# Pooled attention with a top-1 mixture of experts: the zero rows of dropped tokens move to the front of the expert loop, and two steps of the hand-over change places

## Chip, cores and metric

The kernel runs on one core of one Trainium2 chip. The metric is device time in microseconds of one execution. The time given for a kernel is the median of its runs. Times inside an execution are counted from the start of the profiled span.

## What is computed

Attention over pooled keys and values (pool of 8) gives 4608 rows of 512 numbers. A gate of 8 columns picks one expert for each row. Each expert takes at most `capacity` = 1152 rows, in the order of the rows; a row that comes later is dropped, and its output is zero. Kept rows go through two products with a ReLU between and are scaled by their gate weight.

```python
def _moe_ref(x, w_gate, w1, w2, capacity):
    logits = x @ w_gate
    expert_idx = np.argmax(logits, axis=1)
    ...
    for i in range(N):
        e = expert_idx[i]
        if counts[e] < capacity:
            disp[e, counts[e]] = x[i]
            pos[i] = counts[e]
            counts[e] += 1
            keep[i] = True
    h = np.maximum(np.einsum('ecd,edf->ecf', disp, w1), 0.0)
    y = np.einsum('ecf,efd->ecd', h, w2)
    out = np.zeros((N, D), dtype=np.float32)
    for i in range(N):
        if keep[i]:
            out[i] = gate_w[i] * y[expert_idx[i], pos[i]]
```

## The kernel before, in words

The program has three parts.

**Attention.** It works through units of rows, writes the attention rows to `xs` in device memory, routes them as it goes and scatters pairs (row number, gate weight) into `slots`, which is sorted by expert. It ends at about 209 us of the span.

**The prologue (`prologue`, the hand-over).** The expert that has most rows after half of the batch is known early. Its first 256 rows are computed while the last routing steps and the tables of the loop (`tables`) are still being made. The order of its instructions is written out by hand (a block with a manual schedule: each engine takes its instructions in the order of the source). `product(yp[1], ...)` is split in two halves of 12 matmuls, with the transposes of the next rows (`transposed`) between them on TensorE. `load_w2(e1, nc.scalar)` issues the next expert's w2 on ScalarE's queue. Then VectorE makes two versions of the row list: `idd` (the dropped rows alone; all other entries get the number NT = 4608) and `ids` (the kept rows alone). A scatter with bounds check leaves out an entry of NT. `columns(ix1, ...)` copies the two columns of the first pass, `gather(xg, ix1, ...)` on GpSimd fetches their rows, and `finish(i)` (L986 to L988) multiplies `yp[i]` with the gate weight on VectorE and scatters it from GpSimd. In the loop's own pools, `zi` (zeros) and the PSUM tile `y[1]` are then cleared on VectorE (L1111, L1115). PSUM tile `y[1]` lies on the bank of the prologue's `pa`, whose second half is `yp[1]`.

**The loop (L1158).** 20 passes in this execution, counted from 0 here; the number is read from a register. A pass takes up to 256 rows of one expert, in two tiles of 128. With `two` set both tiles are worked on (15 passes, the long ones: `hidden_all` in four groups of 24 matmuls that take turns over three PSUM buffers `ph`, then `product(y[1], ...)`); otherwise only one (5 passes, the short ones: `hidden_one`). Where the expert changes (`sw`), ScalarE and VectorE split the next expert's w1 and w2 into two parts each (`split_w1`, `split_w2`; `split` puts the high part on ScalarE, the low part on VectorE), and where there is one more expert to come (`nw`), SP loads its weights behind that. The order in a pass, for each engine:

- TensorE: hidden layer, `product(y[1])`, transposes of the rows for the next pass, `product(y[0])`.
- VectorE: `hl` of each group (L1133), the w1 split, `ix` (the two columns of the pass after the next), the two `xl`, `io` (this pass's columns), `gate(1)`, `iz` (this pass's columns of dropped rows, L1183), `gate(0)`, the w2 split, and then `hl` of the next pass.
- GpSimd: it clears `io` (L1167) and `iz` (L1168), gathers `xg` (L89, L91), then reads `iz` once into `guard` (L1184) and scatters `zrow` (a tile of zeros) to the rows in `iz` (two scatters, L96), then scatters `ys[1]` and `ys[0]` to the rows in `io` (L1193, L96).

Clearing an index tile on GpSimd, and reading a tile into `guard` or `guardf`, serve the ordering: an instruction that clears `io` waits until the scatters that read `io` have landed, and VectorE's write of `io` then waits for the clearing alone. The same holds for `iz`. SP stores one row of `zrow` into `xs` ahead of the loop (L1155).

All engines make semaphore events at the loop's entry (L1158); a first-pass instruction that depends on what another engine did before the loop waits for that engine's entry event.

```python
            with tc.manual_schedule():
                ...
                nc.gpsimd.tensor_sub(io, zi, zi)
                nc.gpsimd.tensor_sub(iz, zi[:, 0], zi[:, 0])
                ...
                nc.vector.tensor_scalar(out=iz, in0=idd[:, ds(cd, 2)], ...)
                nc.gpsimd.tensor_sub(guard[:, 0], iz, iz)
                for i in range(2):
                    scatter(iz[:, i : i + 1], zrow[:, :], across_iterations=True)
                product(y[0], hh, hl, 0)
                gate(0)
```

Of the kernel before, what the change touches and what calls it, by code (L numbers as in the profile page):

```python
# [12 lines left out]
I32 = mybir.dt.int32  # L13
# [6 lines left out]
DVE = mybir.EngineType.DVE  # L20

P = 128
# [9 lines left out]
def pooled_attn_top1_moe(ctx: ExitStack, tc: tile.TileContext, q, k, v, wg, w1, w2, cap, out):  # L32
# [7 lines left out]
    nc = tc.nc  # L40
# [40 lines left out]
    idd = const.tile([P, NCOL + 2], I32, name="idd")  # L81
    guard = const.tile([P, 2, 2], I32, name="guard")
    guardf = const.tile([P, 2], F32, name="guardf")

    def columns(dst, src):
        nc.vector.tensor_scalar(out=dst, in0=src, scalar1=0, scalar2=None, op0=ALU.bitwise_or)  # L86
# [29 lines left out]
    def load_w2(e, eng=nc.sync, **kw):  # L116
        for c in range(0, KF, 4):
            eng.dma_start(wr[2][:, c : c + 4], rows(w2f, e * DF + c * P, 4 * P).rearrange("(c p) f -> p c f", p=P), **kw)
# [30 lines left out]
    def product(y, hh, hl, i, first=0, last=3 * KF):  # L149

        terms = [(hh, wr["h"]), (hh, wr["l"]), (hl, wr["h"])]
        for n in range(first, last):
            a, b = terms[n // KF]
            c = n % KF
            nc.tensor.matmul(y, a[:, c, i * P : (i + 1) * P], b[:, c], start=(n == 0), stop=(n == 3 * KF - 1))  # L155


    with ExitStack() as actx:
# [558 lines left out]
        with tc.manual_schedule():  # L717
# [102 lines left out]
            def transposed(i, x):  # L820

                p_ = bank([P, KD, P], "pxe", F32R)
                for c in range(KD):
                    nc.tensor.transpose(p_[:, c], x[:, i, c * P : (c + 1) * P], identr)
                s = (slice(None), slice(None), slice(i * P, (i + 1) * P))
                split(xh[s], xl[s], p_.bitcast(F32))
# [105 lines left out]
            def prologue():  # L932

                hh = ld.tile([P, KF, 2 * P], F32R, name="hh", tag="qblk")
                hl = ld.tile([P, KF, 2 * P], F32R, name="hl", tag="qblk")
                pa = pav.tile([P, 2, 512], F32, name="pa", tag="pa")
                pc = [psc.tile([P, 4, 2 * P], F32, name="ps", tag="ps") for _ in range(2)]
                two = [pc[0][:, 0:2], pc[1][:, 0:2], pa[:, 0].rearrange("p (a n) -> p a n", a=2), pc[0][:, 0:2]]
                ya = wk.tile([P, 2, H, D], F32, name="xo", tag="xo").rearrange("p a h d -> p a (h d)")
                yp = [pc[1].rearrange("p a n -> p (a n)")[:, 0:DM], pa[:, 1]]  # L940

                def hidden(g):
                    hidden_two(g, two[g], xh, xl)

                def relu(g):
                    s = (slice(None), slice(2 * g, 2 * g + 2))
                    nc.scalar.activation(hh[s], two[g], AF.Relu)
                    nc.vector.scalar_tensor_tensor(out=hl[s], in0=two[g], scalar=0.0, in1=hh[s].bitcast(F32), op0=ALU.max, op1=ALU.subtract)

                def w2_piece(c, eng):  # L950
                    s = (slice(None), c)
                    split(wr["h"][s], wr["l"][s], wr[2][s], eng)

                drain(dq)
                e1 = nc.values_load(esi[0:1, 1:2], engines=(SP, mybir.EngineType.Activation), min_val=0, max_val=E - 1)
                load_w1(e1)
                hidden(0)
                for c in range(5):
                    w2_piece(c, nc.gpsimd)
                drain(rq)  # L960
                drain(sq)
                ix = sm.tile([P, 2, 2], I32, name="idp", tag="idp", bufs=2)
                nc.sync.dma_start(ix, slotv[:, ds(early["e0"] * MT + 2, 2), :])
                nc.sync.dma_start(ids[:, 0:NCOL, :], slotv)
                rq.append(tables())
                relu(0)
                hidden(1)
                for c in (5, 6, 7):
                    w2_piece(c, nc.vector)
                    step(rq, 4)  # L970
                relu(1)
                hidden(2)
                step(rq, 10)
                relu(2)
                hidden(3)
                nc.vector.tensor_tensor(out=ix[:, :, 0], in0=ix[:, :, 0], in1=mkeep[:, 2:4], op=ALU.max)
                gather(xg, ix, xs[:, :])
                step(rq, 4)
                relu(3)
                product(yp[0], hh, hl, 0)  # L980
                drain(rq)
                ido = sm.tile([P, 2], I32, name="ido", tag="ido", bufs=1)
                idp = early["id"]
                nc.vector.tensor_tensor(out=ido, in0=idp[:, :, 0], in1=mkeep[:, 0:2], op=ALU.max)

                def finish(i):  # L986
                    nc.vector.tensor_scalar_mul(ya[:, i], yp[i], idp[:, i, 1:2].bitcast(F32))
                    scatter(ido[:, i : i + 1], ya[:, i])  # L988

                product(yp[1], hh, hl, 1, 0, 12)  # L990
                for i in range(2):
                    transposed(i, xg)
                load_w2(e1, nc.scalar)
                product(yp[1], hh, hl, 1, 12, 24)
                nc.vector.tensor_tensor(out=idd, in0=ids[:, :, 0], in1=mdrop, op=ALU.max)
                nc.vector.tensor_tensor(out=ids[:, :, 0], in0=ids[:, :, 0], in1=mkeep, op=ALU.max)
                c1 = nc.values_load(cf[0:1, 3, 1:2], engines=(DVE,), min_val=0, max_val=NCOL)
                ix1 = sm.tile([P, 2, 2], I32, name="ix1", tag="ix1", bufs=1)
                columns(ix1, ids[:, ds(c1, 2), :])
                gather(xg, ix1, xs[:, :])  # L1000
                finish(0)
                finish(1)

            NPU = 2 * NB + 1
# [94 lines left out]
    with ExitStack() as bctx:  # L1099
# [6 lines left out]
        ys = [tb.tile([P, DM], F32, name=f"ys{i}") for i in range(2)]  # L1106
        ix = tb.tile([P, 2, 2], I32, name="ix")
        io = tb.tile([P, 2, 2], I32, name="io")
        iz = tb.tile([P, 2], I32, name="iz")
        zi = tb.tile([P, 2, 2], I32, name="zi")  # L1110
        nc.vector.memset(zi, 0)  # L1111
        px = [pp.tile([P, KD, P], F32R, name=f"px{i}") for i in range(2)]
        ph = [pp.tile([P, 512], F32, name=f"ph{i}") for i in range(3)]
        y = [pp.tile([P, DM], F32, name=f"y{i}") for i in range(2)]
        nc.vector.memset(y[1], 0.0)  # L1115

        def transpose_x():
            for i in range(2):
# [39 lines left out]
        with tc.For_i(0, nt, 1, iteration_sync="reg_based") as t:  # L1158
            with tc.manual_schedule():
# [3 lines left out]
                we = nc.values_load(cf[0:1, 2, ds(t, 1)], engines=(SP,), min_val=0, max_val=E - 1)  # L1163
                ct = nc.values_load(cf[0:1, 3, ds(t, 1)], engines=(DVE,), min_val=0, max_val=NCOL)
                c2 = nc.values_load(cf[0:1, 3, ds(t + 2, 1)], engines=(DVE,), min_val=0, max_val=NCOL)
                cd = nc.values_load(cf[0:1, 4, ds(t, 1)], engines=(DVE,), min_val=0, max_val=NCOL)
                nc.gpsimd.tensor_sub(io, zi, zi)  # L1167
                nc.gpsimd.tensor_sub(iz, zi[:, 0], zi[:, 0])  # L1168
                with tc.If(two > 0) as both:
                    hidden_all()  # L1170
# [10 lines left out]
                columns(io, ids[:, ds(ct, 2), :])  # L1181
                gate(1)
                nc.vector.tensor_scalar(out=iz, in0=idd[:, ds(cd, 2)], scalar1=0, scalar2=None, op0=ALU.bitwise_or)  # L1183
                nc.gpsimd.tensor_sub(guard[:, 0], iz, iz)  # L1184
                for i in range(2):
                    scatter(iz[:, i : i + 1], zrow[:, :], across_iterations=True)
                product(y[0], hh, hl, 0)
                gate(0)
                with tc.If(sw > 0):  # L1189
# [31 lines left out]
```

## Time and profile before

| | us |
|---|---|
| Median of 3 runs | 672.89 (671.79 to 673.55) |
| The profiled execution's own time | 671.99 |
| Its span in the trace | 669.8 |
| TensorE busy (matmuls) | 625.5, 93% of the span |
| VectorE busy | 343.9, 51% |
| GpSimd busy | 310.6, 46% |
| ScalarE busy | 236.8, 35% |
| Mean granted TensorE clock | 0.981 |

The own time is 2.2 us longer than the span: work around the first and the last instruction that the trace does not show. Busy time is the union of an engine's instructions. In the rows, PE is TensorE, DVE VectorE, ACT ScalarE, POOL GpSimd, and a q behind a name is the engine's sequencer; L146 is line 146 of the kernel; `out<-in` are the tiles; what stands in square brackets is the idle time of the engine before the instruction, and what ended it.

### The profile page before, as it was taken

How to read it: one execution, taken by the hardware profiler on the slowest of the kernel's cores; microseconds unless marked ns; L12 is line 12 of the kernel's file. 1: busy time of each engine (PE TensorE's matmuls, PEld its weight loads, DVE VectorE, ACT ScalarE, POOL GpSimd, SP SyncE). 2: the span in 40 equal slices, each digit the busy share in tenths (PEclk: the TensorE clock that was granted, in tenths of full speed). 3: DMA queues.
4: the chain of work that ended last, by engine and by line, in shares of the span. 5: the costliest groups of instructions: out<-in, count | busy, mean ns of one | idle time of the engine just before them, and what ended most of it. 6: DMA issues, size and time to landing. Idle time of an engine off the chain costs nothing. (4 is left out here: it accounts for less than half of the span.)

```text
span 669.8 us, 14743 instructions
## 1 busy us (share of the span) xinstructions
PE 625.5 (93%) x4218; PEld 560.6 (84%) x4219; DVE 343.9 (51%) x783; ACT 236.8 (35%) x401; POOL 310.6 (46%) x467
## 2 busy tenths in 40 slices
PE   2899989999878989999999999999999999999994
PEld 2899879888777878997888899897998978989983
DVE  4466767778778832227826642224622466221222
ACT  2455545556454111215616431124311463111111
POOL 7699952543386323135543444313543056431444
PEclk9799989999899989999999999999999999999998
DMA  9994844344273151014843761101711181110112
GB/s 326 372 385 138 322 158 127 126 155 145 81 244 120 47 192 31 31 63 171 325 152 142 252 253 63 31 31 63 289 63 31 35 300 38 63 31 31 63 47 64
DMA packets 47086, 93.82 MB, mean 140 GB/s; under 512 B 13392, under 2 KB 23632, under 8 KB 47060
## 3 DMA queue, kind: packets, MB, share of 16 engines
q1 hardware_dynamic: 30836, 60.37, 25.9%
q0 software_dynamic: 11392, 21.57, 9.8%
q10 hardware_dynamic: 4832, 11.56, 4.5%
q8 instruction: 13, 0.21, 0.1%
q14 instruction: 13, 0.11, 0.1%
HBM read 132.97 MB, written 31.27 MB: 245 GB/s over the span
## 5 line engine op out<-in xcount | busy, mean ns | idle before, releaser
L1132 ACT ACTIVATE hh<-ph 128x512 fp32r<-128x512 f32 x60 | 35.9, 599 | 181.3 <-PE ph L146 169.7
L1133 DVE SCALAR_TENSOR_TENSOR hl<-ph,hh 128x512 fp32r<-128x512 f32 x60 | 41.0, 691 | 110.8 <-ACT hh L1132 47.6
L146 PE MATMUL ph<-xl,w1h 128*128 128x256 f32 x480 | 76.8, 282 | 2.6 <-DVE io L86 2.6
L146 PE MATMUL ph<-xh,w1h 128*128 128x256 f32 x480 | 76.9, 282 | 2.1 <-DVEq L1158 2.1
L146 PE MATMUL ph<-xh,w1l 128*128 128x256 f32 x480 | 76.5, 281 | 0.0
L155 PE MATMUL y<-w2h,hh 128*128 128x512 f32 x280 | 72.3, 400 | 0.0
L155 PE MATMUL y<-w2h,hl 128*128 128x512 f32 x280 | 71.0, 396 | 0.0
L155 PE MATMUL y<-w2l,hh 128*128 128x512 f32 x280 | 71.0, 396 | 0.0
L146 PEld LDWEIGHTS ph<-xh,w1h 128*128 128x128 f32 x480 | 66.7, 190 | 3.8 <-issue 2.5
L91 POOL DMA_INDIRECT xg<-xs,ix x42 | 41.1, 978 | 61.8 <-PE y L155 52.3
L146 PEld LDWEIGHTS ph<-xl,w1h 128*128 128x128 f32 x480 | 65.4, 189 | 3.3 <-issue 3.3
L146 PEld LDWEIGHTS ph<-xh,w1l 128*128 128x128 f32 x480 | 65.5, 190 | 0.0
L485 PE MATMUL pa<-vbd,pT 96*128 96x146 f32 (+1 forms) x480 | 63.1, 296 | 1.7 <-DVE lt L511 1.5
L155 PEld LDWEIGHTS y<-w2h,hl 128*128 128x128 f32 x280 | 52.6, 188 | 12.7
L155 PEld LDWEIGHTS y<-w2l,hh 128*128 128x128 f32 x280 | 52.6, 188 | 12.7
L89 POOL TENSOR_TENSOR guard<-ix 128x4 int32<-128x4 int32 x21 | 4.1, 197 | 122.6 <-DVE ix L86 77.5
L485 PEld LDWEIGHTS pa<-vbd,pT 96*128 96x128 f32 (+1 forms) x480 | 58.0, 186 | 3.0 <-ACT pT L472 2.4
L155 PEld LDWEIGHTS y<-w2h,hh 128*128 128x128 f32 x280 | 50.0, 188 | 9.4
L1153 DVE TENSOR_SCALAR ys<-y,io 128x512 f32<-128x512 f32 x40 | 30.0, 751 | 48.9 <-PE y L155 43.7
L122 DVE TENSOR_TENSOR xl<-px,xh 128x512 fp32r<-128x512 f32 x40 | 25.7, 685 | 56.4 <-ACT xh L121 56.4
L96 POOL DMA_INDIRECT out_dram<-zrow,iz x40 | 47.4, 1184 | 14.8 <-issue 13.6
L472 ACT COPY pT<-pp 96x384 f32<-96x384 f32 x72 | 33.9, 475 | 45.3 <-PE pp L471 44.2
(256 smaller groups left out, 1095.0 us busy)
## 6 DMA issues: line engine op xcount, KB each, us to landing
r<-in_moe_w_dram SPq DMA_DIRECT2D x84, 1024.0 KB, 10.9
raw<-in_k_dram SPq DMA_DIRECT2D x12, 768.0 KB, 7.4
raw<-in_v_dram SPq DMA_DIRECT2D x12, 768.0 KB, 9.4
xs<-xo ACTq DMA_DIRECT2D x16, 512.0 KB, 2.8
qblk<-in_q_dram SPq DMA_DIRECT2D x14, 512.0 KB, 6.0
raw<-in_moe_w_dram SPq DMA_DIRECT2D x4, 512.0 KB, 5.2
r<-in_moe_w_dram ACTq DMA_DIRECT2D x2, 1024.0 KB, 8.5
qblk<-in_q_dram SPq DMA_DIRECT2D x4, 256.0 KB, 8.1
```

The source lines that it names most:

```text
L89: nc.gpsimd.tensor_sub(guard, ix, ix)
L91: nc.gpsimd.indirect_dma_start(out=dst[:, i, :].bitcast(F32), out_offset=None, in_=src, in_offset=bass.IndirectOffsetOnAxis(ap=ix[:, i, 0: ...
L96: ins = nc.gpsimd.indirect_dma_start(out=out[:, :], out_offset=bass.IndirectOffsetOnAxis(ap=i_, axis=0), in_=src, in_offset=None, bounds_c ...
L122: eng.tensor_sub(lo, src, hi.bitcast(F32))
L146: nc.tensor.matmul(p[:, f2], a[:, c, f * P : (f + 1) * P], b[:, c], start=(f2 == 0 and j == 0 and c == 0), stop=(f2 == 1 and j == 2 and c ...
L155: nc.tensor.matmul(y, a[:, c, i * P : (i + 1) * P], b[:, c], start=(n == 0), stop=(n == 3 * KF - 1))
L472: nc.scalar.copy(self.pT[:, j], pp[0:KC, 0:HC])
L485: nc.tensor.matmul(self.pa[us, j, h0 * XW : (h0 + 2) * XW], self.pT[:, j, c, us], vbd[b % 2][:, cc].rearrange("r a x -> r (a x)"), start=( ...
L1132: nc.scalar.activation(hh[s], p, AF.Relu)
L1133: nc.vector.scalar_tensor_tensor(out=hl[s], in0=p, scalar=0.0, in1=hh[s].bitcast(F32), op0=ALU.max, op1=ALU.subtract)
L1153: nc.vector.tensor_scalar_mul(ys[i], y[i], io[:, i, 1:2].bitcast(F32))
```

## The change

In the prologue, `finish(0)` and the making of `idd`, `ids` and `ix1` move ahead of the transposes, the load and the second half of the product; the gather follows the load; and a copy of the first pass's columns of dropped rows into `iz` is new. `iz` becomes a tile of the outer pool. In the loop, the two scatters of zero rows move from behind `gate(1)` to the pass's front, ahead of the clearing of `iz`, with a one-column memset of `zrow` and two guards (three instructions; the guard of `iz` moves with them). VectorE's write of `iz` stays where it is and takes the columns of the next pass (`t + 1`). `zi` is cleared on GpSimd, and `y[1]` by a ScalarE copy of `zrow`.

```diff
+    iz = const.tile([P, 2], I32, name="iz")
@@ prologue
                 product(yp[1], hh, hl, 1, 0, 12)
-                for i in range(2):
-                    transposed(i, xg)
-                load_w2(e1, nc.scalar)
-                product(yp[1], hh, hl, 1, 12, 24)
+                finish(0)
                 nc.vector.tensor_tensor(out=idd, in0=ids[:, :, 0], in1=mdrop, op=ALU.max)
                 nc.vector.tensor_tensor(out=ids[:, :, 0], in0=ids[:, :, 0], in1=mkeep, op=ALU.max)
                 c1 = nc.values_load(cf[0:1, 3, 1:2], engines=(DVE,), min_val=0, max_val=NCOL)
                 ix1 = sm.tile([P, 2, 2], I32, name="ix1", tag="ix1", bufs=1)
                 columns(ix1, ids[:, ds(c1, 2), :])
+                for i in range(2):
+                    transposed(i, xg)
+                load_w2(e1, nc.scalar)
                 gather(xg, ix1, xs[:, :])
-                finish(0)
+                c0 = nc.values_load(cf[0:1, 4, 0:1], engines=(DVE,), min_val=0, max_val=NCOL)
+                columns(iz, idd[:, ds(c0, 2)])
+                product(yp[1], hh, hl, 1, 12, 24)
                 finish(1)
@@ ahead of the loop
-        iz = tb.tile([P, 2], I32, name="iz")
         zi = tb.tile([P, 2, 2], I32, name="zi")
-        nc.vector.memset(zi, 0)
+        nc.gpsimd.memset(zi, 0)
...
-        nc.vector.memset(y[1], 0.0)
+        nc.scalar.copy(y[1], zrow)
@@ in the loop
-                cd = nc.values_load(cf[0:1, 4, ds(t, 1)], engines=(DVE,), min_val=0, max_val=NCOL)
+                cd = nc.values_load(cf[0:1, 4, ds(t + 1, 1)], engines=(DVE,), min_val=0, max_val=NCOL)
                 nc.gpsimd.tensor_sub(io, zi, zi)
+
+                nc.gpsimd.memset(zrow[:, 0:1], 0.0)
+                nc.gpsimd.tensor_sub(guardf, zrow[:, 0:2], zrow[:, 0:2])
+                nc.gpsimd.tensor_sub(guard[:, 0], iz, iz)
+                for i in range(2):
+                    scatter(iz[:, i : i + 1], zrow[:, :], across_iterations=True)
                 nc.gpsimd.tensor_sub(iz, zi[:, 0], zi[:, 0])
...
                 nc.vector.tensor_scalar(out=iz, in0=idd[:, ds(cd, 2)], scalar1=0, scalar2=None, op0=ALU.bitwise_or)
-                nc.gpsimd.tensor_sub(guard[:, 0], iz, iz)
-                for i in range(2):
-                    scatter(iz[:, i : i + 1], zrow[:, :], across_iterations=True)
                 product(y[0], hh, hl, 0)
```

## Rows read from the trace of the kernel before

**Rows 1.** Busy time by stage: stretch, length, busy us of each engine (instructions), PEclk, DMA.

```profile
238.70:244.30 5.60, 3.51 (x18) 3.53 (x18) 1.97 (x5) 0.00 (x0) 3.85 (x5) 0.70 0.89 310
...
244.30:661.00 416.70, 412.55 (x2585) 365.67 (x2584) 171.84 (x265) 122.35 (x176) 159.92 (x236) 1.00 0.31 108
```

**Rows 2.** What TensorE waits for in the loop: us in total, times, longest.

```profile
PE ph L146 <- DVE io L86: 2.6, 4, 0.9
PE ph L146 <- DVEq L1158: 2.1, 1, 2.1
```

**Rows 3.** TensorE at the hand-over: start us, us, engine, line, operation [idle before].

```profile
236.67 2.04 PE L155 MATMUL pa<-w2h,hl 128*128 128x512 f32 x8
240.80 1.09 PE L146 MATMUL ph<-xh,w1h 128*128 128x256 f32 x4 [2.09 <-DVEq L1158]
```

**Rows 4.** VectorE at the hand-over, in order of time.

```profile
237.59 0.46 DVE L996 TENSOR_TENSOR ids<-ids,mkeep 128x290 int32<-128x290 int32 x1
...
239.43 0.74 DVE L987 TENSOR_SCALAR xo<-pa,idp 128x512 f32<-128x512 f32 x1
...
240.36 0.48 DVE L1115 MEMSET y<- 128x512 f32 x1 [0.17 <-DVE zi L1111]
```

**Rows 5.** The loop's first line: sequencer events, count, ns, first and last start.

```profile
L1158 ACTq EVENT_SEMAPHORE  x2: 17/17/17, 238.2 to 238.3; - x2
L1158 DVEq EVENT_SEMAPHORE  x2: 21/21/21, 240.6 to 240.7; - x2
```

**Rows 6.** Busy time and granted clock (PEclk) behind two stalls of TensorE.

```profile
240.80:244.30 3.50, 3.50 (x17) 3.50 (x18) 0.04 (x1) 0.00 (x0) 2.69 (x3) 0.52 0.88 297
328.50:332.00 3.50, 3.50 (x32) 3.50 (x31) 3.50 (x5) 0.60 (x1) 3.14 (x3) 1.00 1.00 405
```

**Rows 7.** The tail: GpSimd's last scatters and VectorE's last gate.

```profile
652.02 0.99 POOL L96 DMA_INDIRECT out_dram<-ys,io  x1 [2.15 <-issue]
...
661.08 0.75 DVE L1153 TENSOR_SCALAR ys<-y,io 128x512 f32<-128x512 f32 x1 [2.18 <-PE y L155]
...
664.40 0.99 POOL L96 DMA_INDIRECT out_dram<-ys,io  x1 [0.16 <-issue]
```

**Rows 8.** GpSimd across the seam of two usual passes.

```profile
412.55 0.99 POOL L96 DMA_INDIRECT out_dram<-ys,io  x1 [0.16 <-issue]
415.44 0.19 POOL L1167 TENSOR_TENSOR io<-zi 128x4 int32<-128x4 int32 x1 [1.89 <-DMA out_dram<-ys,io]
...
423.82 0.20 POOL L89 TENSOR_TENSOR guard<-ix 128x4 int32<-128x4 int32 x1 [8.01 <-DVE ix L86]
```

**Rows 9.** The scatters' line: issue to landing.

```profile
DMA to landing us min/median/max: 2.1/2.7/8.0
```

**Rows 10.** GpSimd across the seam of passes 2 and 3.

```profile
314.26 1.79 POOL L96 DMA_INDIRECT out_dram<-ys,io  x1 [0.16 <-issue]
...
316.53 1.79 POOL L96 DMA_INDIRECT out_dram<-ys,io  x1 [0.15 <-issue]
323.49 1.15 POOL L1167 TENSOR_TENSOR io<-zi 128x4 int32<-128x4 int32 x1 [5.17 <-DMA out_dram<-ys,io]
```

**Rows 11.** VectorE in pass 3.

```profile
321.10 4.62 DVE L122 TENSOR_TENSOR w1l<-r,w1h 128x1024 fp32r<-128x1024 f32 x4
...
327.85 0.16 DVE L1183 TENSOR_SCALAR iz<-idd 128x2 int32 x1
...
333.11 1.28 DVE L1133 SCALAR_TENSOR_TENSOR hl<-ph,hh 128x512 fp32r<-128x512 f32 x2
```

**Rows 12.** Busy time and DMA share in pass 3.

```profile
325.70:331.80 6.10, 5.32 (x45) 5.14 (x44) 5.99 (x11) 3.19 (x4) 4.80 (x6) 1.00 0.97 352
```

**Rows 13.** TensorE, start of the fourth group of pass 4.

```profile
334.81 0.64 PE L146 MATMUL ph<-xh,w1h 128*128 128x256 f32 x4
```

**Rows 14.** Pass 14: GpSimd's clearing of io, VectorE's write of iz.

```profile
552.99 1.20 POOL L1167 TENSOR_TENSOR io<-zi 128x4 int32<-128x4 int32 x1 [6.35 <-DMA out_dram<-ys,io]
...
556.27 0.16 DVE L1183 TENSOR_SCALAR iz<-idd 128x2 int32 x1
```

## The prediction

> **What bounds the kernel now.** I read the stages first, then what TensorE waits for, then the two seams that the diff touches, then GpSimd's queue inside the loop. In the loop, TensorE is busy 412.6 of 416.7 us at full granted clock [rows 1]: it is the bound there, and whatever leaves it fed costs nothing. Of its few stalls, 2.6 us in four pieces wait for VectorE, and one of 2.1 us stands at the hand-over [rows 2]. So three places can move the end: the hand-over, the tail behind the last matmul, and any pass in which another engine newly makes TensorE wait.
>
> The change removes no matmul and no transfer. Counting the reference's routing over its inputs, one expert of eight is over capacity, with 236 dropped rows; they lie in the column pairs of passes 4 and 5 (counted from 0). All other zero-row scatters carry row numbers out of bounds and write nothing, but are issued and waited for all the same.
>
> **Hand-over.** The last product of the prologue ends at 236.67+2.04 = 238.71; the loop's first matmul starts at 240.80 [rows 3]. In between VectorE runs finish(0), finish(1) and two memsets, having come from the ids [rows 4]; its loop-entry semaphore event comes at 240.7, and TensorE goes 0.1 us later, while ScalarE's entry event was given at 238.3 [rows 5]. From the start of the last VectorE instruction (240.36) to TensorE's start it is 0.44 us: a register load and the events.
> After the change finish(0) (as long as finish(1), 0.74), the two instructions over all ids (0.46 each) and both column copies with their register loads, some 3 us in all, run while TensorE is still at the product. I cost them at nothing; their cover is the product's end at 238.71, and what of them were still to run then would push finish(1) by as much. finish(1) then runs 238.8 to 239.6. By VectorE alone TensorE could start at 238.8+0.44 = 239.2. But y[1] lies over the PSUM tile that finish(1) reads: in the program of before the memset of y[1] waits for finish(1). Now a ScalarE copy has that wait, and TensorE's first matmul waits for ScalarE's entry event as well. The copy starts at about 239.7, so TensorE at about 239.7+0.44+0.15 (one more wait) = 240.3. **Gain 0.5** (bounds 0.4 and 1.6). The zi memset on GpSimd runs behind its scatter and its landing is not awaited by TensorE. The gather and the first scatter go some 3 us earlier on GpSimd; the gather is read only in mid-pass, 15 us on.
> The granted clock: after the 2.1 us idle, TensorE ran 3.5 us at a mean 0.52, almost all of it at the 1.2 GHz level, and made about half of its work [rows 6], so 0.52 costs 3.5x(1-0.52) = 1.7 us. With 1.6 us idle it may stay at 2.4 GHz. I leave this 1.7 in and keep its loss as a bound.
>
> **Tail.** In the last pass the two zero-row scatters stand on GpSimd ahead of the two result scatters; gate(0) ends at 661.08+0.75 = 661.83, but the last result scatter starts only at 664.40 [rows 7]. With the zero rows gone it could start 0.4 us behind gate(0), at 662.2: gain 2.2. It comes later if the gather ahead of it does, which now stands behind the front's chain: zero scatter, landing, clearing of iz. If GpSimd's own 2 us pause ahead of the scatter in the pass before [rows 7] comes again, the chain ends that much later and the gain falls to 0.3. I take the middle, **1.3**.
>
> **The loop's front.** Every pass now issues on GpSimd ahead of the gather: clearing io, zrow memset, two guards, two zero scatters, clearing iz. Clearing iz has to wait until the zero scatters have landed, since they read iz; VectorE's write of iz waits for that clearing, and behind it in VectorE's queue stand gate(0), the w2 split and the next pass's hl. SP's queue is passed by none of it but the one-row store of zrow, which the memset of the first pass awaits; nothing hurries there.
> In a usual pass there is room: clearing io 2.9 us behind the last result scatter, and 8 us more until the gather's guard gets its ix [rows 8]; the chain needs three reads of 0.2, two scatters 1.3 apart and a landing of 2.7, the median [rows 9], some 5 us. Free, therefore, in 18 passes: the long ones, and the short ones whose front is not under a weight load.
> Pass 3 is short and follows a pass whose w2 load delays the result scatters. Its io clearing waits until 323.49, which is 7.0 us after the second scatter at 316.53; the one that is left at 314.26 lands, by the same 7.0, at 321.3 [rows 10]. From there VectorE splits w1 from 321.10 to 325.7 [rows 11], and GpSimd's clearing took 1.15 there instead of 0.19 [rows 8, 10]. Three reading instructions: 321.3+3.45 = 324.7; two scatters of about 1.4 with 0.3 between: the second starts at 326.6.
> Its landing is not in the trace of before. The bounds are the median of 2.7 and the 7.0 under a load; at 325.7 to 331.8 the next w1 load holds the DMA engines at 0.97 [rows 12]. The scatter writes no rows here, so I take 4.3, nearer to the lower end: 330.9, iz cleared at 331.1. VectorE wants to write iz at 327.85 [rows 11] and loses 3.2 us. Its first hl of the next pass ends at 333.11+0.7 = 333.8, and TensorE's fourth group, which needs that PSUM buffer, starts at 334.81 [rows 13]: slack 1.0. **TensorE stalls 2.2** (bounds 0, if the front's instructions are not held up, and 4.9).
> Pass 14 is the same picture: io cleared at 552.99, iz written at 556.27 [rows 14]. With one scatter fewer in the load's way io comes about 2.3 earlier; three reads 3.45, a scatter 1.3, a landing of 2.1 without load [rows 9]: iz cleared at 557.8, 1.5 late, less slack 1.0: **0.5** (bounds 0 and 1.5).
>
> The memset of one column of zrow reads nothing; no row shows it under a split, so its bounds are 0.1 and 1.15, and I took 0.1. The Trainium skill (SBUF — State Buffer, "SBUF: two separate sides") has it that a VectorE instruction with two SBUF inputs locks out only a GpSimd instruction that reads SBUF. By that rule the memset stays at 0.1 and the stall at 2.2; without it the stall is 3.2.
>
> **Sum.** -0.5 -1.3 +2.2 +0.5 = +0.9 on the profiled execution's own 671.99, so 672.9. That execution lies 0.9 under the median of the runs, 672.89; on that scale 673.8.
>
> **Rivals.**
> 1. *No new stall:* the scatters of the front land before VectorE comes to iz. For it: they move no data, and GpSimd is idle 5 us there. Against: result scatters under the same loads took 7 us. Then -0.5-1.3 = -1.8, and with the clock held at the hand-over up to -3.5: 671.1 to 669.4, middle 670.3. The Trainium skill (DMA: Bandwidth & Descriptors, "SWDGE vs HWDGE vs iDMA") speaks for this rival: each DMA engine goes round its queues, so a small software scatter should not wait for a load to end. The trace disagrees in so far as scatters landed 7 us late under loads [rows 10].
> 2. *Slower, by the clock:* the stall of pass 3 is long enough for the granted clock to fall behind it, as after the 2.1 us at the hand-over; after the stalls of at most 0.9 us [rows 2], one of which lies in this pass, it did not fall [rows 6]. Point of decision: an idle of some 2 us. Price 1.7, and with a landing nearer 5 than 4.3 another 0.7: 673.8+2.4 = 676.2, at most 678.5.
> 3. *ScalarE does not hold TensorE:* the copy into y[1] does not wait for finish(1); then TensorE starts at 239.2, the idle is 0.5, the clock stays: 1.1+1.7 better than the sum, 671.0. Against it is the wait of the memset.
>
> **Numbers.** Forecast 0.36, rival 1 0.30, rival 2 0.26, rival 3 0.08. A measurement of this kernel tells 0.3%, 2.0 us, from no change: below 670.9 or above 674.9. Faster: seven tenths of rival 1 and most of rival 3, 0.27. Slower: nearly all of rival 2 and a tenth of the forecast's own spread, 0.29. Within: 0.44. Range 669.3 to 677.6: rival 1 with the clock held, down to rival 2 short of its extreme; the forecast's own range is 672.0 to 675.5.
>
> **What would show it.** Right: TensorE's first loop matmul 1.4 to 1.8 us behind the product, behind ScalarE's copy; the last scatter 0.3 to 2.2 us earlier against gate(0); a new wait of GpSimd's iz clearing for the zero scatters in every pass, and in passes 3 and 14 of VectorE's iz write for GpSimd, with TensorE idle 1 to 3 us some 6 us later. Wrong: no VectorE wait at iz (rival 1), a low clock behind pass 3 (rival 2), the first matmul at 0.5 us (rival 3), or gathers that come late to the transposes, which I cost at nothing because 10 us lie between them.

## The result, and the profile after

The changed kernel takes **678.25 us** (median of 4 runs, 677.91 to 679.03), before 672.34 beside it: ratio **1.0113**, 95% interval 1.0084 to 1.0142. The forecast was 673.8, the range 669.3 to 677.6. The profiled execution's span is 676.3 against 669.8, its own time 677.91.

The stages tell where the 6.5 us of span lie. I cut both traces at events that both have: the end of the prologue's last product, TensorE's first matmul of the loop, the first transposes of each pass, the end of the last matmul, the last landing. First the changed kernel's windows (stretch, length, busy us of PE, PEld, DVE, ACT, POOL with instructions, granted clock, DMA share, GB/s): the idle at the hand-over, from there to the transposes of pass 0, from the transposes of pass 3 to those of pass 4, of pass 14 to those of 15, and from the last matmul to the last landing.

```profile
237.20:238.67 1.47, 0.00 (x1) 0.03 (x1) 0.75 (x1) 0.59 (x1) 0.82 (x3) 1.00 1.05 389
238.67:255.73 17.06, 17.06 (x120) 15.94 (x121) 2.94 (x5) 2.39 (x4) 3.66 (x9) 1.00 0.34 123
315.66:347.86 32.20, 25.89 (x154) 23.27 (x153) 15.99 (x22) 11.53 (x15) 14.36 (x20) 0.89 0.58 208
551.90:577.17 25.27, 23.82 (x155) 21.22 (x153) 15.99 (x22) 11.53 (x15) 14.93 (x21) 1.00 0.29 101
...
666.43:673.57 7.14, 0.00 (x0) 0.00 (x0) 0.75 (x1) 0.00 (x0) 4.43 (x6) 0.72 0.43 111
```

The same windows of the kernel before:

```profile
238.71:240.80 2.09, 0.00 (x1) 0.03 (x1) 1.92 (x5) 0.00 (x0) 1.16 (x2) 1.00 0.90 331
240.80:259.27 18.47, 18.47 (x120) 17.34 (x121) 2.98 (x6) 2.40 (x4) 3.57 (x6) 0.91 0.32 116
318.89:343.25 24.36, 23.58 (x154) 21.19 (x153) 15.95 (x22) 11.54 (x15) 11.93 (x15) 1.00 0.79 285
547.21:571.68 24.47, 23.58 (x155) 21.19 (x153) 15.94 (x22) 11.54 (x15) 11.00 (x15) 1.00 0.32 106
...
660.98:667.11 6.13, 0.00 (x0) 0.00 (x0) 0.75 (x1) 0.00 (x0) 3.73 (x6) 0.76 0.30 85
```

| Stage, us | Before | After | Difference |
|---|---|---|---|
| Up to the product's end | 238.71 | 237.20 | -1.51 |
| TensorE idle at the hand-over | 2.09 | 1.47 | -0.62 |
| From there to pass 0's transposes | 18.47 | 17.06 | -1.41 |
| Pass 3 to pass 4 | 24.36 | 32.20 | **+7.84** |
| Pass 14 to pass 15 | 24.47 | 25.27 | +0.80 |
| Last matmul to last landing | 6.13 | 7.14 | +1.01 |
| All other passes and the end, together | | | +0.4 |

The first line is no effect of the change. All that the diff moves in the prologue lies in the last 6 us ahead of the product's end. TensorE's last idle ahead of that stretch ends 23.6 to 23.7 us before the product's end in both kernels, here before and then after:

```profile
215.03 0.39 PE L604 MATMUL po<-su,chigh 128*128 128x8 f32 x2 [0.69 <-DVE su L600]
```

```profile
213.59 0.39 PE L605 MATMUL po<-su,chigh 128*128 128x8 f32 x2 [0.69 <-DVE su L601]
```

So 1.44 of the 1.51 us are there already. (One and the same kernel, the hand-over's part alone, run below on two chips, had its product's end at 244.20 in one profile and at 236.93 in the other.) I therefore compare kernels from the product's end to the end of the span: **431.1 before, 439.1 after**, 8.0 more, which lies inside the 5.6 to 9.5 us that the ratio's interval gives.

What TensorE waits for inside the loop (us in total, times, longest) answers to [rows 2]:

```profile
PE ph L147 <- DVE hl L1135: 5.7, 2, 5.3
PE ph L147 <- DVE io L87: 3.0, 4, 1.0
```

The wait of 5.3 for hl is new; the waits for io were there. Its cause is read backwards in pass 3. GpSimd there, in order of time, answers to [rows 10]:

```profile
318.31 1.05 POOL L1169 TENSOR_TENSOR io<-zi 128x4 int32<-128x4 int32 x1 [5.48 <-DVE hl L123]
319.29 0.09 POOL L1171 MEMSET zrow<- 128x1 f32 x1
319.46 1.02 POOL L1172 TENSOR_TENSOR guardf<-zrow 128x2 f32<-128x2 f32 x1
320.45 1.18 POOL L1173 TENSOR_TENSOR guard<-iz 128x2 int32<-128x2 int32 x1
321.78 1.80 POOL L97 DMA_INDIRECT out_dram<-zrow,iz  x1 [0.15 <-issue]
323.88 0.98 POOL L97 DMA_INDIRECT out_dram<-zrow,iz  x1 [0.30 <-issue]
331.02 0.19 POOL L1176 TENSOR_TENSOR iz<-zi 128x2 int32<-128x2 int32 x1 [6.16 <-DMA out_dram<-zrow,iz]
```

VectorE in the same pass answers to [rows 11]:

```profile
324.19 0.75 DVE L1155 TENSOR_SCALAR ys<-y,io 128x512 f32<-128x512 f32 x1
331.25 0.17 DVE L1191 TENSOR_SCALAR iz<-idd 128x2 int32 x1 [6.30 <-POOL iz L1176]
331.33 0.75 DVE L1155 TENSOR_SCALAR ys<-y,io 128x512 f32<-128x512 f32 x1
332.00 4.62 DVE L123 TENSOR_TENSOR w2l<-r,w2h 128x1024 fp32r<-128x1024 f32 x4
336.53 1.88 DVE L1135 SCALAR_TENSOR_TENSOR hl<-ph,hh 128x512 fp32r<-128x512 f32 x3
```

Read it upwards: hl at 336.53 stands behind the w2 split, this behind gate(0), this behind a write of two integers per partition that waited 6.30 us for the clearing of iz, which waited 6.16 for the zero scatters to land. The second scatter took 323.88 to 330.86, 7.0 us, to write nothing. TensorE's fourth group, and behind it the granted clock (the window has the columns of the first fence), answer to [rows 13, 6]:

```profile
337.27 1.22 PE L147 MATMUL ph<-xh,w1h 128*128 128x256 f32 x4 [5.32 <-DVE hl L1135]
```

```profile
335.10:341.90 6.80, 4.63 (x21) 4.63 (x22) 3.31 (x5) 0.00 (x0) 3.80 (x5) 0.50 0.89 287
```

So of the 7.84 us, 5.32 are the stall; TensorE's busy time for the same matmuls rises from 23.58 to 25.89, and these 2.31 are the clock, at 1.2 GHz for 6.8 us. In no other stretch of the loop did it fall.

Why the landing took 7 us shows in the DMA queues, first of 323.9 to 326.4, then of 326.4 to 329.2 (queue, kind: packets, MB, share of 16 engines). q1 carries the weight load, issued at 321.8 and 322.9; q0 is GpSimd's:

```profile
q1 hardware_dynamic: 267, 1.03, 100.8%
```

```profile
q1 hardware_dynamic: 230, 0.88, 78.5%
q0 software_dynamic: 155, 0.00, 3.1%
```

For 2.5 us all 16 engines carry the load alone, and the scatters' packets go only as it thins out. VectorE stood idle for 5.9 of the second scatter's 7.0 us, so it was not the splits that held these packets. In pass 6 both scatters are issued just ahead of a load, which is issued at 385.67 and sends its first packet at 386.8. The first scatter was issued at 384.16, and its packets went at 385.7 to 385.9, ahead of the load's. The second was issued at 385.46, and from 386.8 to 390.6 only the load's packets went (issues from 384 to 385, and from 385.3 to 386, KB each, us to landing):

```profile
out_dram<-zrow,iz POOLq DMA_INDIRECT x1, 2.1
```

```profile
r<-in_moe_w_dram SPq DMA_DIRECT2D x1, 1024.0 KB
out_dram<-zrow,iz POOLq DMA_INDIRECT x1, 7.4
```

VectorE waited 4.5 us for iz there as well, but in a long pass, whose slack took it: TensorE has no new wait there.

**The hand-over**, against [rows 3, 4]:

```profile
237.24 0.75 DVE L988 TENSOR_SCALAR xo<-pa,idp 128x512 f32<-128x512 f32 x1 [1.26 <-PE pa L156]
...
238.03 0.59 ACT L1117 COPY y<-zrow 128x512 f32<-128x512 f32 x1 [3.07 <-DVE xo L988]
...
238.67 0.71 PE L147 MATMUL ph<-xh,w1h 128*128 128x256 f32 x4 [1.47 <-ACT y L1117]
```

TensorE now waits for finish(1) and ScalarE's copy, 1.47 us, and the clock behind it stays at full: 17.06 us to the transposes instead of 18.47.

**The tail**, GpSimd across the last seam, against [rows 7]:

```profile
657.53 1.02 POOL L97 DMA_INDIRECT out_dram<-ys,io  x1 [3.21 <-issue]
660.46 0.19 POOL L1169 TENSOR_TENSOR io<-zi 128x4 int32<-128x4 int32 x1 [1.92 <-DMA out_dram<-ys,io]
...
662.93 0.98 POOL L97 DMA_INDIRECT out_dram<-zrow,iz  x1 [0.30 <-issue]
665.19 0.19 POOL L1176 TENSOR_TENSOR iz<-zi 128x2 int32<-128x2 int32 x1 [1.28 <-DMA out_dram<-zrow,iz]
...
666.71 0.99 POOL L92 DMA_INDIRECT xg<-xs,ix  x1 [0.58 <-PE y L156]
...
670.79 1.02 POOL L97 DMA_INDIRECT out_dram<-ys,io  x1 [0.16 <-issue]
```

The gather, which VectorE's ix at 661.97 would have let go, comes behind the landing and the clearing, 0.3 us after TensorE's end, where before it stood 3.3 ahead:

```profile
657.65 0.98 POOL L91 DMA_INDIRECT xg<-xs,ix  x1 [0.65 <-PE y L155]
```

What follows is shorter by two scatters, 2.7 us, so the 3.6 us of delay leave the last scatter 4.4 us behind TensorE's end instead of 3.4.

### The profile page after: what moved, and what is told of

Read it like the earlier page. It is cut to its first block, busy times and chain, and to the rows that moved or that the text cites. A ratio compares the mean times of both kernels' runs of the same rounds, so it can differ in the third digit from the quotient of the medians.

```text
span 676.3 us, 14845 instructions
## 1 busy us (share of the span) xinstructions
PE 625.6 (93%) x4218; PEld 560.6 (83%) x4219; DVE 343.4 (51%) x782; ACT 237.6 (35%) x402; POOL 318.3 (47%) x508
## 4 chain that ended last, share of the span: by engine, by line
PE 77%; DMA 5%; DVE 5%; ACT 4%; issue 4%; POOL 2%; DVEq 1%; POOLq 0%; ACTq 0%; SPq 0%
PE y L156 26%; PE ph L147 23%; PE pa L486 8%; PE ps L449 4%; PE ph L1145 3%; PE pk L383 3%; PE pp L472 3%; PE pq L434 2%; PE px L1122 2%; ACT kbs L392 2%; DMA slots<-pairs,gix 1%; ACT w1h L122 1%; DMA out_dram<-ys,io 1%; PE pv L410 1%; DMA out_dram<-zrow,iz 1%
## 5 line engine op out<-in xcount | busy, mean ns | idle before, releaser
L92 POOL DMA_INDIRECT xg<-xs,ix x42 | 45.6, 1086 | 49.3 <-PE y L156 39.1
L486 PE MATMUL pa<-vbd,pT 96*128 96x146 f32 (+1 forms) x480 | 61.1, 291 | 1.7 <-DVE lt L512 1.5
L486 PEld LDWEIGHTS pa<-vbd,pT 96*128 96x128 f32 (+1 forms) x480 | 56.3, 182 | 3.1 <-ACT pT L473 2.4
L97 POOL DMA_INDIRECT out_dram<-ys,io x40 | 45.7, 1141 | 17.4 <-issue 17.4
L449 PE MATMUL ps<-kbs,qT 128*128 128x144 f32 x256 | 46.9, 310 | 2.1 <-ACT qT L435 2.1
```

The lines of the kernel that those rows point to most:

```text
L92: nc.gpsimd.indirect_dma_start(out=dst[:, i, :].bitcast(F32), out_offset=None, in_=src, in_offset=bass.IndirectOffsetOnAxis(ap=ix[:, i, 0: ...
L97: ins = nc.gpsimd.indirect_dma_start(out=out[:, :], out_offset=bass.IndirectOffsetOnAxis(ap=i_, axis=0), in_=src, in_offset=None, bounds_c ...
L449: nc.tensor.matmul(self.ps[:, h, 0 : 2 * SP_].rearrange("p (a x) -> p a x", a=2), self.qT[:, h], kbs[self.b % 2][:, :, self.hf * HH + h], ...
L486: nc.tensor.matmul(self.pa[us, j, h0 * XW : (h0 + 2) * XW], self.pT[:, j, c, us], vbd[b % 2][:, cc].rearrange("r a x -> r (a x)"), start=( ...
```

## The experiments

The theory: the loss is VectorE's iz write in pass 3, which hands the landing under a load on to all that stands behind it. Rivals: GpSimd's own lateness under the splits, and for each smaller term one of its own. In the table, "way" is from transposes to transposes, "tail" from the last matmul to the last landing, "all" from the product's end to the end of the span; us of one profile each. e1 and e9, the same kernel, differ by 0.5 in the tail, and kernels with the same old loop differ by up to 0.6 on the way from 14 to 15, so differences of this size mean nothing there. Ratios are to the kernel before on the same chip; e5 to e8 and e11 were run once, and they are read by their stages alone.

| Kernel | Idle at hand-over | Way 3 to 4 | Way 14 to 15 | Tail | All |
|---|---|---|---|---|---|
| before | 2.09 | 24.36 | 24.47 | 6.1 | 431.1 |
| after | 1.47 | 32.20 | 25.27 | 7.1 | 439.1 |
| e1 hand-over alone | 1.47 | 24.40 | 24.91 | 6.6 | 429.9 |
| e2 zero rows alone | 2.89 | 32.65 | 25.17 | 7.1 | 442.5 |
| e3 staged columns | 1.47 | 24.20 | 24.43 | 7.0 | 430.7 |
| e4 no zero rows | 1.59 | 24.29 | 24.41 | 5.0 | 433.2 |
| e5 load of w1 held | 1.47 | 25.29 | 25.31 | 7.8 | 434.2 |
| e6 clearing late | 1.59 | 30.33 | 28.20 | 6.6 | 441.0 |
| e7 a gather more | 1.59 | 32.34 | 25.23 | 7.2 | 439.3 |
| e8 iz write last | 1.60 | 28.16 | 24.86 | 7.3 | 434.4 |
| e9 as e1 | 1.59 | 24.30 | 25.05 | 6.1 | 429.7 |
| e10 y[1] freed | 0.62 | 24.61 | 24.43 | 6.1 | 428.4 |
| e11 a scatter more | 1.47 | 32.14 | 25.29 | 7.2 | 439.5 |

**e1, the hand-over's part alone.** The diff's hunks on the prologue, zi and y[1], without the first columns of iz; the loop is that of before. The cut shows the prologue against the changed kernel.
```diff
                 load_w2(e1, nc.scalar)
                 gather(xg, ix1, xs[:, :])
-                c0 = nc.values_load(cf[0:1, 4, 0:1], engines=(DVE,), min_val=0, max_val=NCOL)
-                columns(iz, idd[:, ds(c0, 2)])
                 product(yp[1], hh, hl, 1, 12, 24)
```

> Before, with the hand-over's part of the change alone (finish(0) and the ids ahead, y[1] cleared by ScalarE, zi by GpSimd); the loop is that of before. Theory: the gain that the changed kernel shows up to pass 3 belongs to this part and comes by two steps, TensorE idle 1.5 us instead of 2.1 between the product and the loop (0.6) and no low clock behind it (1.4 on 3.4 us): 2.0 faster than before, span near 667.8, ratio 0.997. The profile of the changed kernel is another 1.5 ahead already at the product's end; if that too belongs to the change, 3.5 faster, 0.995. Rival: the low clock behind the hand-over comes and goes from execution to execution, whatever the idle; then 0.6, ratio 0.999. No TensorE wait over 1 us inside the loop by any theory.

Ratio 0.9955 (0.9925 to 0.9985). Its windows, idle and then up to the transposes:

```profile
244.20:245.67 1.47, 0.01 (x1) 0.04 (x1) 0.75 (x1) 0.59 (x1) 0.40 (x1) 1.00 1.02 391
245.67:262.73 17.06, 17.06 (x121) 15.94 (x122) 2.94 (x5) 2.40 (x4) 1.21 (x4) 1.00 0.32 116
```

Both steps stand, to the hundredth. The ratio's interval, 1.0 to 5.1 us, holds the 2.0 of the two steps and the 3.5 that would include the 1.5 ahead of the product's end; that the 1.5 doesn't belong to the change rests on the two rows in the result's section. In all nine further kernels with an idle of 0.6 to 1.6 here the clock held.

**e2, the zero rows' part alone.** The loop is the changed one; the cut shows the prologue against the kernel before.
```diff
+                c0 = nc.values_load(cf[0:1, 4, 0:1], engines=(DVE,), min_val=0, max_val=NCOL)
+                columns(iz, idd[:, ds(c0, 2)])
                 finish(0)
                 finish(1)
```

> Before, with the zero rows' part of the change alone (scatters at the loop's front, first columns read at the end of the prologue); the hand-over is that of before. Theory: VectorE's iz write in pass 3 waits some 6 us for zero scatters that land 7 us after their issue under a weight load, TensorE stalls 5.3 and runs 6.8 us at the low clock (2.5), pass 14 loses 0.8, the tail 1.0: 9.6 slower than before, ratio 1.014. Rival: part of the loss comes from the two parts together (the gather and first scatters earlier on GpSimd); then nearer 1.010.

Ratio 1.0139 (1.0112 to 1.0166). TensorE's waits:

```profile
PE ph L147 <- DVE hl L1135: 6.0, 2, 5.5
PE ph L147 <- DVEq L1160: 2.9, 1, 2.9
```

The whole loss sits in this part. The extra copy on VectorE's way through the old hand-over costs 0.8 more, where the change as a whole hides it under the product.

**e3, the columns staged on GpSimd.**
```diff
+                nc.gpsimd.tensor_add(zs, iz, zi[:, 0])
                 nc.gpsimd.memset(zrow[:, 0:1], 0.0)
                 nc.gpsimd.tensor_sub(guardf, zrow[:, 0:2], zrow[:, 0:2])
-                nc.gpsimd.tensor_sub(guard[:, 0], iz, iz)
                 for i in range(2):
-                    scatter(iz[:, i : i + 1], zrow[:, :], across_iterations=True)
-                nc.gpsimd.tensor_sub(iz, zi[:, 0], zi[:, 0])
+                    scatter(zs[:, i : i + 1], zrow[:, :], across_iterations=True)
```

> The changed kernel with one thing more: GpSimd copies the columns into a tile of its own ahead of the scatters, which read that copy, so the clearing of iz and with it VectorE's wait for the landing go away. The two scatters stay where they are, the reads ahead of them are one fewer. Theory (the landing under the load, passed on through the clearing): no VectorE wait at iz, the 5.3 of pass 3 and the 2.5 of clock go, pass 14's 0.8 goes, and the gather no longer stands behind a landing, which gives up to 2.3 in the tail: span 665 to 668, faster than before, ratio 0.993 to 0.997. Rival (GpSimd itself is late, held up by the splits, and everything behind the scatters on its queue with it): the stall of pass 3 stays within 2 us of what it was, ratio 1.005 or more.

Ratio 0.9983 (0.9957 to 1.0008). Pass 3 is as before, though its front was as late as ever (three reads of 1.0 to 1.3 us under the split, second scatter 8.3 us behind the transposes, as in the changed kernel):

```profile
322.09:346.29 24.20, 23.52 (x155) 21.10 (x154) 15.95 (x22) 11.53 (x15) 12.85 (x17) 1.00 0.80 277
```

So in the loop neither the scatters nor GpSimd's lateness cost anything by themselves; the wait that was tied to them did. The whole kernel missed its theory of 0.993 to 0.997, because the tail kept the 7.0 of the changed kernel and gained nothing. The gathers went ahead in time, but gate(0) started 1.86 us behind the last matmul's end instead of 0.11, and the same (1.82) is seen in e6, the other kernel with the gathers 2.1 us ahead of that end. The trace shows what gate(0) waited for: TensorE's signal, whose last record stands at 666.74, 1.76 behind the end that the profile gives the last matmul (before, 0.02). In both kernels the last matmuls' signals come in bunches up to 1.4 us apart, where before they come every 0.23. Matmul ends are modelled in these profiles, so it isn't shown whether the matmuls or only their signals were late, nor why.

**e4, without the zero rows.**
```diff
-                nc.gpsimd.memset(zrow[:, 0:1], 0.0)
-                nc.gpsimd.tensor_sub(guardf, zrow[:, 0:2], zrow[:, 0:2])
-                nc.gpsimd.tensor_sub(guard[:, 0], iz, iz)
-                for i in range(2):
-                    scatter(iz[:, i : i + 1], zrow[:, :], across_iterations=True)
```

> The changed kernel without the two zero-row scatters and the memset and reads ahead of them; the 236 rows of dropped tokens are not written, the clearing of iz and VectorE's iz write stay. Theory: the scatters cost nothing but the wait at iz and the delay of the gather; so within 1 us of the kernel with the staged copy, 664.5 to 667. Rival: the scatters cost by themselves (DMA contention, GpSimd's time): over 1.5 us faster than the staged one.

Ratio 1.003 (0.9995 to 1.0064), so not faster than e3, and 2.5 us slower from the product's end, where the theory gave 1. The loop agrees with e3 within 0.1 in passes 3 and 14: there the rival falls. But this span ends 7.2 us behind the last landing, where the others end 2.6 to 2.7 behind it. These 4.5 us are GpSimd's closing instruction on its sequencer (DRAIN), which takes 8.25 us here and 4.11 in the changed kernel; why, the trace doesn't show. Without them e4 would be 2.0 faster than e3, all of it in the tail (5.0 against 7.0): e3 has GpSimd's pause (see e7) and gate(0)'s late start there, and e4 has neither.

**e5, the load of w1 held back.**
```diff
+                nc.gpsimd.memset(wr[1][:, 0, 0:1], 0.0)
+                nc.gpsimd.memset(wr[1][:, 2, 0:1], 0.0)
                 load_w1(we, cond=nw > 0, bounds_check="skip_entire_dma")
```

> The changed kernel, where in every pass the load of w1 waits for GpSimd's clearing of iz (two one-column memsets by GpSimd into the load's buffer), so that no weight load runs while the zero scatters land. Everything else stays, GpSimd's reads under the splits too. Theory (the scatter is slow because the load's packets are ahead of it): the two scatters of pass 3 land 2 to 3 us after their issue instead of 7.0 to 7.3, VectorE's wait at iz falls from 6.3 to about 2, TensorE's stall from 5.3 to 0.5 to 1.1, the clock stays at full, the way from pass 3's transposes to pass 4's is 24.9 to 25.5 us instead of 32.2. Rival (the scatter is slow by itself, beside VectorE's splits): it still lands after some 7 us and the way stays near 32.

Of the instructions on iz: who waited (us, times), and the landings.

```profile
  DVE iz L1193: 8.2, 5
...
DMA to landing us min/median/max: 2.1/2.1/3.1
```

In the changed kernel these read 13.7 and 2.1/2.1/7.4. In pass 3 the reads took 1.02 and 1.18 and the first scatter 1.80 as there, but the second landed 2.1 us behind its issue, VectorE's wait for iz fell to 1.4, and the way is 25.29. The load was the cause, the splits weren't. Holding the load costs 1.1 us between passes 5 and 6, so it is a test and not a remedy.

**e6, the clearing one place later.** The line leaves the front.
```diff
                 gather(xg, ix, xs[:, :])
+                nc.gpsimd.tensor_sub(iz, zi[:, 0], zi[:, 0])
                 split_x()
```

> The changed kernel with the clearing of iz one place later on GpSimd, behind the gather. It tells the tail's term from pass 3's. Theory: pass 3 keeps its loss (32 us from transposes to transposes), since the clearing waits for the same landing; in the last pass the gather no longer stands behind the landing and the last scatter starts 1.5 to 2 us earlier, 5.2 to 5.7 us from TensorE's end to the last landing instead of 7.14. Rival (the tail is late by GpSimd's pause in the pass before alone): 6.5 or more.

The theory of the tail missed: 6.6, the rival's number. The gathers did go ahead, 2.1 us before the last matmul's end, and gate(0) was late as in e3, so the number doesn't show the rival's mechanism. And the move was not free. The iz write now waits for the gathers too, which wait for TensorE:

```profile
  DVE iz L1191: 17.5, 9
```

The way from pass 14 to 15 grew to 28.20: TensorE idled 1.85 us, and the clock fell behind it.

```profile
580.44 0.74 PE L147 MATMUL ph<-xh,w1h 128*128 128x256 f32 x4 [1.85 <-DVE hl L1135]
```

```profile
581.94:585.35 3.41, 3.41 (x16) 3.24 (x15) 0.00 (x0) 0.60 (x1) 1.07 (x2) 0.50 0.02 0
```

**e7 and e11, one GpSimd DMA more in the prologue:** a gather into a spare tile (e7), or a scatter out of bounds (e11).
```diff
                 gather(xg, ix, xs[:, :])
+                nc.gpsimd.indirect_dma_start(out=spare[:, :], out_offset=None, in_=xs[:, :],
+                                             in_offset=bass.IndirectOffsetOnAxis(ap=ix[:, 0, 0:1], axis=0))
```
```diff
                 gather(xg, ix, xs[:, :])
+                nc.gpsimd.memset(nowhere, 2 * NT)
+                nc.gpsimd.tensor_sub(guard[:, 0, 0:1], nowhere, nowhere)
+                scatter(nowhere, zrow[:, :])
```

> The changed kernel with one idle gather more on GpSimd in the prologue, into a tile nobody reads. In all kernels of 164 GpSimd DMAs so far the 158th waits 2.1 to 3.2 us for nothing that the trace shows; it is the second result scatter of the last pass but one. Theory (the pause goes by the count of GpSimd's DMAs): now the 158th is the first result scatter of that pass, which has 3 us to spare; the second starts under 1 us behind gate(0) instead of 3.5, and the last pass's chain on GpSimd with it: 4.2 to 5 us from TensorE's end to the last landing instead of 7.14. Rival (the pause belongs to that place in the loop): it stays on the second scatter, 7.1.

> The changed kernel with one more scatter on GpSimd in the prologue, of zero rows to row numbers out of bounds, which writes nothing. A gather more did not move GpSimd's pause in the last pass but one. Theory (the pause goes by the number of scatters alone): it moves to the first result scatter, the second starts about 1 us behind gate(0) instead of 3.5. Rival (it belongs to the place in the loop, or to the gathers there): 3.5 again, and the way from TensorE's end to the last landing stays 7.1.

Both rivals hold. e7, the last pass but one:

```profile
665.98 1.02 POOL L98 DMA_INDIRECT out_dram<-ys,io  x1 [3.21 <-issue]
```

In every kernel but e4 this scatter starts 8.9 to 9.0 us ahead of the last matmul's end; with the loop of before it shows as 2.1 us idle [rows 7] only because GpSimd was busy up to then. In e4 it starts 11.5 ahead, after 0.7 idle. The cause of the pause stays open.

**e8, the iz write last in VectorE's pass.** The line leaves its place ahead of gate(0).
```diff
                 with tc.If(sw > 0):
                     split_w2()
+                nc.vector.tensor_scalar(out=iz, in0=idd[:, ds(cd, 2)], scalar1=0, scalar2=None, op0=ALU.bitwise_or)
                 load_w2(we, cond=nw > 0, bounds_check="skip_entire_dma")
```

> The changed kernel with VectorE's iz write moved behind gate(0) and the w2 split, the last thing it does in a pass. The landing under the load stays at 7 us. Theory (what costs is what is queued behind the write, not the write itself): gate(0) and the split run while the scatters land, the write waits under 1.5 us, TensorE's stall of pass 3 is under 0.7, the way from pass 3's transposes to pass 4's 24.3 to 25.1 us, pass 14's 24.4 to 24.6. Rival (TensorE waits for something else that the scatters hold up): 28 or more.

The way is 28.16: the theory missed by 3 us, though the write itself waited only 0.1. VectorE:

```profile
333.55 4.62 DVE L123 TENSOR_TENSOR w2l<-r,w2h 128x1024 fp32r<-128x1024 f32 x4
338.25 0.17 DVE L1195 TENSOR_SCALAR iz<-idd 128x2 int32 x1
342.24 1.88 DVE L1135 SCALAR_TENSOR_TENSOR hl<-ph,hh 128x512 fp32r<-128x512 f32 x3 [3.82 <-issue]
```

The 3.82 us ahead of hl are the loop's entry on VectorE's sequencer: five loads of registers and their checks. In the changed kernel the same chain ran 332.4 to 336.4, under the w2 split. A wait behind the split holds the sequencer, and the entry comes into the open. The number is the rival's, but it is VectorE's own entry that TensorE waits for, and nothing else that the scatters hold up. So not only the instructions behind a wait count, but the register work that the sequencer would have done ahead.

**e9 and e10, y[1] freed.** e9 is e1 again, beside e10, which has:
```diff
-        px = [pp.tile([P, KD, P], F32R, name=f"px{i}") for i in range(2)]
+        y = [pp.tile([P, DM], F32, name=f"y{i}") for i in range(2)]
         ph = [pp.tile([P, 512], F32, name=f"ph{i}") for i in range(3)]
-        y = [pp.tile([P, DM], F32, name=f"y{i}") for i in range(2)]
+        px = [pp.tile([P, KD, P], F32R, name=f"px{i}") for i in range(2)]
```

> Before with the hand-over's part of the change alone, a second time and on the same chip as the next kernel, to be compared with it. Theory as in the first: TensorE idle 1.5 us, clock at full behind it, the way from the product's end to pass 0's transposes 18.5 us against 20.6 of before; ratio to before 0.995 to 0.998.

> The same, with the PSUM tiles of the loop allocated in another order (y, ph, px instead of px, ph, y), so that y[1] no longer lies over the tile that finish(1) reads, and ScalarE's copy into it need not wait. Theory (ScalarE's copy behind finish(1) is what ends TensorE's wait last): the copy runs under the product, TensorE starts 0.5 to 0.9 us behind the product instead of 1.5, by VectorE's entry into the loop; 0.6 to 1.0 us faster than the kernel beside it, the fastest of all so far. Rival (VectorE's entry would end the wait at the same time anyway): 1.4 to 1.5, no difference.

e9 0.9965 (0.994 to 0.999), e10 0.9968 (0.9943 to 0.9992). Idle and way to the transposes in e10:

```profile
237.27:237.89 0.62, 0.00 (x0) 0.03 (x1) 0.58 (x1) 0.00 (x0) 0.56 (x2) 1.00 1.06 390
237.89:254.82 16.93, 16.93 (x120) 15.81 (x121) 3.11 (x6) 2.39 (x4) 1.61 (x4) 1.00 0.39 136
```

In the trace the idle falls by 0.97 as expected; in the times the two can't be told apart. Both intervals lie below 1 and below that of the changed kernel.

## Why the prediction was wrong

**Pass 3, the step that failed: the landing.** The prediction put +2.2 with "I take 4.3, nearer to the lower end", because the scatter writes no rows, although it had the next load at a DMA share of 0.97 beside it [rows 12]. It took 7.0, the upper bound, which was the one number of the trace that came from beneath a load [rows 10]. Bytes were the wrong ground: the 8-byte packets landed as late behind a load as the whole rows of rows 10 (7.0 and, in pass 6, 7.4), and in 2.1 without one (e5). The stall of TensorE that hangs on it was 5.3, not 2.2. All else in this step held: from the clearing of io to the first scatter 3.5 us (3.45 forecast), the second scatter 0.5 later than forecast if the 3.2 us by which the pass comes earlier are counted, the slack 1.0 (6.3 late, 5.3 stalled). The memset took 0.09 under the split, the reads 1.02 to 1.18. This agrees with the Trainium skill (SBUF — State Buffer, "SBUF: two separate sides"), by which a VectorE instruction with two SBUF inputs locks out only a GpSimd instruction that reads SBUF.

**The clock, a rival that came true.** Rival 2 had the mechanism and a price of 1.7 for a stall of about 3; at 5.3 it cost 2.3. "An idle of some 2 us" as the point of decision was wrong: e8 idled 3.1 in pass 3 and its clock stayed at 1.00, e6 idled 1.85 in pass 14 and its clock fell, and at the hand-over 2.1 (before) and 2.9 (e2) were enough. Ahead of both e8's and e6's idle TensorE had worked 7.8 us without a gap, so neither the length of the idle nor the work ahead of it decides alone; what does, these runs don't show. Rival 2's extreme of 678.5 came near the measured 678.25 partly by luck: the tail's miss of 2.3 is made up by the 1.4 of clock gained at the hand-over and the 1.5 ahead of the product's end, which is not the change's.

**Rival 1** (no new stall) fell with the landing. The Trainium skill (DMA: Bandwidth & Descriptors, "SWDGE vs HWDGE vs iDMA") has each engine go round its queues, which would have let the scatters through. The trace doesn't bear it out here: no GpSimd packet went for 2.5 us of a load at 100.8%. Whether the packets stood behind the load's or weren't there yet, no run tells.

**Pass 14:** +0.5 forecast, 0.8 measured; the iz write waited 1.4, of which 0.42 came through to TensorE. e1 and e9, with the old loop, have 0.4 and 0.6 more than before in this pass too, so part of the 0.8 is not shown to be the change's.

**The tail failed in its sign:** -1.3 forecast, +1.0 measured. The middle of two bounds was taken where the chain could be summed: clearing of io 2.9 us behind the last scatter [rows 7, 8], so 654.9; and from there the chain takes 10.3 (measured; two scatters, a landing, two gathers, two scatters), 665.2 against 664.40. The chain was named in the prediction and not added up, and the pause on GpSimd was there in both kernels, so nothing was won by it.

**The hand-over** was right: -0.62 where -0.5 was forecast, behind ScalarE's copy (e10 shows that the copy, and not VectorE, ends the wait; rival 3 was rightly low). The clock's 1.4 was kept as a bound and would have belonged in the sum: e1 and e9 have it each time. That could not be read from the trace of before alone.

**The sum** was +0.9 on the whole kernel; from the product's end it is -0.6 -1.4 +7.8 +0.8 +1.0 and 0.4 spread over all other passes, 8.0.

## What to carry to other kernels

Before an issue moves to another place, ask what runs on the DMA engines at that place, and then who waits for the landing: behind a load an empty scatter lands as late as a full one, and that is paid in full if a buffer comes free only with its landing. A wait is priced by all that stands behind it in its engine's queue, the register work of the next loop pass included, and a copy of a few bytes into a tile of its own (e3) takes the wait away where moving it (e6, e8) only shifts it. Add up the whole chain of the last pass before booking a gain in the tail.

## What the runs showed of the hardware

In pass 6 of the changed kernel a scatter of 8-byte packets landed in 2.1 us when its packets went ahead of a load's, and in 7.4 when it was issued 1.3 us later and they went behind. An idle of TensorE of 1.85 us lowered the clock once (e6), one of 3.08 did not (e8). GpSimd's last scatter of the last pass but one pauses 3.2 us in all eight kernels with zero rows at the front, whatever the count of its DMAs (e7, e11), and 2.1 in the four with the old loop; the cause is open. The prologue of one kernel ended 7.3 us apart on two chips (e1, e9), nearly as much as the change did in all: only stages cut at common events could be compared.
